# Landmark attention and an MLP on one core: a matrix engine order written in the program, fp32 loads with engine casts, landmark sums by matmul

## The chip, the cores and the metric

One core of a Trainium2 chip runs the whole program. The metric is the device time of one execution in microseconds. A core has a matrix engine (TensorE, "PE" in the rows, with "PEld" for its weight loads), a vector engine (VectorE, "DVE"), a scalar engine (ScalarE, "ACT"), a general engine (GpSimd, "POOL") and a queue engine that issues transfers (SyncE, "SP"). Every engine runs its own instructions in the order in which they stand in its queue and waits for others by semaphores.

## What is computed

For each of 8 batches and 8 heads of 576 tokens with 64 features, the kernel computes a softmax attention through 32 landmarks, which are means over 18 neighbouring tokens each; then a layer norm and an MLP of 512 to 2048 to 512 features on the 4608 token rows.

```python
q_lm = q.reshape(B, H, 32, 18, D).mean(axis=3)
k_lm = k.reshape(B, H, 32, 18, D).mean(axis=3)
A, Bm, C = sm(q, k_lm), sm(q_lm, k_lm), sm(q_lm, k)      # softmax of scaled products
Z = Bm.T / (norm1(Bm) * norminf(Bm) + 1e-6)
for _ in range(6):
    Z = 2 * Z - Z @ Bm @ Z
x = (A @ Z @ C @ v)                                      # heads side by side: 512 features
xn = (x - mean(x)) / sqrt(var(x) + 1e-6) * g_ln
out = x + relu(xn @ w_ch1) @ w_ch2
```

## The kernel before

A batch is one call of `attention_batch` (L197). Its 576 tokens of 8 heads come as two half-sets (`u` = 0, 1) of four heads. The steps are the same for every batch:

- **Loads.** q and k are fetched by GpSimd-issued transfers that cast fp32 to fp16 on the way (`natq` L64, `natk` L68). v comes in fp32 through SyncE into `vstg` (L140) and GpSimd casts it into `natv` (L144). Loads for a batch are issued one batch ahead.
- **Sums and transposes.** VectorE adds each landmark's tokens (`nsk` L209, `nsq` L214, two of each per batch). TensorE transposes the raw q and k in 36 matmuls per batch (`pst`, L188 in the helper `TR`), VectorE copies them to `kT`, `qT` (L226), and a few matmuls bring the sums into the transposed layout (`pslm`), from which VectorE makes `klm` and `qbd` (L239, L242).
- **Landmark block.** `psb` (landmark by landmark products) is exponentiated by ScalarE (`ebm`), normalised by VectorE (`rsum`, `rcr`, `bm`, `bmT`), and gives `pscs`, `pse` and the start `st` of the iteration. `psc` gives the scores of landmarks against all keys, ScalarE exponentiates them into `ect` (12 instructions per batch), and `pscv` multiplies them with v.
- **Iteration.** Six rounds: 8 small matmuls into `psn`, then one VectorE instruction for the next `st` (L321). Then `pszc` and `zcbd` (L331).
- **Token scores and output.** `psa`, exponentiated into `ea`; `psy` (10 matmuls per batch) times `zcbd`, divided by VectorE into the fp32 rows `xblk` (L361).

The MLP works on groups of four blocks of 128 rows (`moe_group`, nine groups): statistics by VectorE (`bn_stats`, L384), `lnv` and `rstd` on ScalarE, the normalised `xn` by GpSimd (L395), 16 transposes into `psxt` with VectorE copies to `xnT` (L401), 64 matmuls of 512 columns into `psh` with 16 ScalarE evictions `hT` (L409), 64 matmuls of 512 columns into `pso`, and per block an addition `ot` on VectorE (L417) and stores.

The matmuls go through the helper `MM`, so nearly all have the line L184. The program writes attention of batch b and then, from batch 2 on, group b-2; a scheduler is free to reorder every engine's queue by what it expects to be ready, TensorE's too. On-chip accumulators are two pools: five buffers shared by all attention steps, and three (`psM`) shared by `psxt`, `psh` and `pso`.

The weight w1 comes in four 1 MB pieces through SyncE and ScalarE scales and casts them (L157); w2 comes cast by a GpSimd-issued transfer (L161).

Of the kernel before, what the change touches and what calls it, by code (L numbers as in the profile page):

```python
# [15 lines left out]
P = 128  # L16
# [3 lines left out]
def kernel(  # L20
# [22 lines left out]
    NCK = SEG // 2  # L43
# [11 lines left out]
    anat = ctx.enter_context(tc.tile_pool(name="anat", bufs=2))  # L55

    def load_qk(b, split):
        natq = anat.tile([P, U, SEG * D], FP16, name="natq", tag="natq")  # L60
        natk = anat.tile([P, H // 2, 9 * D], FP16, name="natk", tag="natk")
        step = 1 if split else U
        for u in range(0, U, step):
            nc.gpsimd.dma_start(  # L64
                out=natq[:, u:u + step, :],
                in_=q[b, 4 * u:4 * (u + step)].rearrange(
                    "(u h) (l j) d -> (h l) u (j d)", u=step, j=SEG))
            nc.gpsimd.dma_start(  # L68
                out=natk[:, 2 * u:2 * (u + step), :],
                in_=k[b, 4 * u:4 * (u + step)].rearrange(  # L70
                    "(r e) (t j) d -> (e t) r (j d)", e=2, j=9))
        return natq, natk

    nat_tiles = {0: load_qk(0, True)}
# [40 lines left out]
    ect_buf = []  # L115
    zcbd_buf = []
    for i in range(NV):
        t = const.tile([P, H // 2, 9, D + 1], FP16, name=f"natv{i}")
        nc.gpsimd.memset(t[:, :, :, D:D + 1], 1.0)
        natv_buf.append(t)  # L120
        ects = []
        zcs = []
        for u in range(U):
            e_ = const.tile([P, SEG, 2, LM], FP16, name=f"ect{i}{u}")
            nc.gpsimd.memset(e_[0:64, :, 1, :], 0.0)
            nc.gpsimd.memset(e_[64:128, :, 0, :], 0.0)
            ects.append(e_)
# [3 lines left out]
        ect_buf.append(ects)  # L131
        zcbd_buf.append(zcs)

    vstage = ctx.enter_context(tc.tile_pool(name="vstage", bufs=2))

    def load_v(b):
        natv = natv_buf[b % NV]
        for r in range(0, H // 2, 2):
            stg = vstage.tile([P, 2, 9, D], FP32, name="vstg", tag="vstg")
            nc.sync.dma_start(  # L140
                out=stg[:],
                in_=v[b, 2 * r:2 * r + 4].rearrange("(r e) (t j) d -> (e t) r j d",
                                                    e=2, j=9))
            nc.gpsimd.tensor_copy(out=natv[:, r:r + 2, :, 0:D], in_=stg[:])  # L144
        return natv

    v_tiles = {0: load_v(0)}

    g_sb = wpool.tile([P, KCH], FP32, name="g_sb")
    nc.sync.dma_start(out=g_sb[:], in_=moe_g_ln.rearrange("(c p) -> p c", p=P))  # L150
    w1_16 = wpool.tile([P, KCH, HID], FP16, name="w1_16")
    w2_16 = wpool.tile([P, MCH, DM], FP16, name="w2_16")
    with tc.tile_pool(name="wstage", bufs=2) as wstage:
        for c in range(KCH):
            stg = wstage.tile([P, HID], FP32, name="w1stg", tag="w1stg")
# [12 lines left out]
    asm = ctx.enter_context(tc.tile_pool(name="asm", bufs=3))

    xpool = ctx.enter_context(tc.tile_pool(name="xpool", bufs=22))  # L170
    mstat = ctx.enter_context(tc.tile_pool(name="mstat", bufs=4))
    mxn = ctx.enter_context(tc.tile_pool(name="mxn", bufs=2))
    mxnT = ctx.enter_context(tc.tile_pool(name="mxnT", bufs=2))
    mhT = ctx.enter_context(tc.tile_pool(name="mhT", bufs=1))
    mout = ctx.enter_context(tc.tile_pool(name="mout", bufs=2))

    ps1 = ctx.enter_context(tc.tile_pool(name="ps1", bufs=5, space=bass.MemoryType.PSUM))
    psM = ctx.enter_context(tc.tile_pool(name="psM", bufs=3, space=bass.MemoryType.PSUM))

    def pt(shape, dtype, name):  # L180
        return ps1.tile(shape, dtype, name=name, tag="p1")

    def MM(o, l, r, rb=0, cb=0, start=True, stop=True, skip=False):
        nc.tensor.matmul(o, l, r, start=start, stop=stop, tile_position=(rb, cb),  # L184
# [277 lines left out]
```

## Time and profile before

| | us |
|---|---|
| median of three runs | 458.29 |
| lowest and highest | 458.02, 458.29 |
| profiled execution, its own time | 456.55 |
| span of the profiled execution | 454.7 |
| TensorE busy in the span | 367.4 |
| VectorE busy | 237.0 |
| ScalarE busy | 141.5 |
| GpSimd busy | 69.1 |
| mean granted TensorE clock | 0.97 of full |

The span is the time from the first to the last instruction of the core; the profiled execution's own time is 1.85 us more. Busy times of engines overlap. A matmul's duration in the rows contains its pipeline, so neighbouring ones overlap, and the pace is read from the starts.

### The profile page before, as it was taken

What the parts mean: (1) busy time and instruction counts of PE and PEld (TensorE: products, weight loads), DVE (VectorE), ACT (ScalarE), POOL (GpSimd) and SP (SyncE); (2) the same over time, 40 slices, a digit from 0 to 9 for tenths busy, and PEclk for the clock granted to TensorE, in tenths of its full rate; (3) what the DMA queues carried; (4) which work ended last, traced back from release to release, by engine and by line L of the source; (5) the groups of instructions that cost most, each with busy time, mean ns of one, the idle gap of its engine ahead of it and who ended that gap; (6) DMA issues with size and microseconds to landing.
All of it is one profiled execution on the core that took longest, in us unless ns stands there. A gap on an engine that the chain in (4) does not pass through costs nothing.

```text
span 454.7 us, 7489 instructions
## 1 busy us (share of the span) xinstructions
PE 367.4 (81%) x2968; PEld 180.1 (40%) x2968; DVE 237.0 (52%) x598; ACT 141.5 (31%) x303; POOL 69.1 (15%) x102
## 2 busy tenths in 40 slices
PE   1124066798995899699978998999899899899995
PEld 1022034354353345334543455346444444444442
DVE  3546679788787673866286726634473201102001
ACT  1333013147103540354025504530552160350520
POOL 8512102312112100320042002000200200200000
PEclk9999998599998999999989999999899999999999
DMA  9999706306226303630270020003000201102002
GB/s 202 326 309 253 192 1 105 106 10 150 76 54 121 105 1 79 120 105 0 72 127 1 2 69 25 2 16 78 1 1 25 69 0 48 46 1 69 25 23 70
DMA packets 20946, 35.08 MB, mean 77 GB/s; under 512 B 3504, under 2 KB 9648, under 8 KB 20400
## 3 DMA queue, kind: packets, MB, share of 16 engines
q1 hardware_dynamic: 12368, 23.08, 16.8%
q0 software_dynamic: 8544, 11.54, 15.1%
q8 instruction: 23, 0.38, 0.3%
q14 instruction: 11, 0.09, 0.1%
HBM read 36.70 MB, written 9.44 MB: 101 GB/s over the span
## 4 chain that ended last, share of the span: by engine, by line
PE 59%; DMA 18%; DVE 11%; issue 6%; ACT 2%; POOL 2%; SPq 0%; POOLq 0%; DVEq 0%
PE pso L184 27%; PE psh L184 23%; DMA natq<-in_q_dram 8%; DMA natk<-in_k_dram 4%; DVE nsq L214 4%; DMA w1stg<-in_moe_w_ch_dram 3%; DVE nsk L209 2%; PE psy L184 2%; DMA vstg<-in_v_dram 2%; PE psn L184 2%; POOL xn L395 2%; PE pst L188 1%; PE psxt L188 1%; DVE kT L226 1%; DVE xnT L401 1%
## 5 line engine op out<-in xcount | busy, mean ns | idle before, releaser
L184 PE MATMUL psh<-xnT,w 128*128 128x512 f16 x576 | 148.9, 390 | 5.3 <-DVE xnT L401 5.3
L184 PE MATMUL pso<-w,hT 128*128 128x512 f16 x576 | 127.9, 379 | 0.0
L409 ACT ACTIVATE hT<-psh 128x512 f16<-128x512 f32 x144 | 86.0, 597 | 125.2 <-PE psh L184 124.6
L417 DVE TENSOR_TENSOR ot<-pso,xblk 128x512 f32<-128x512 f32 x36 | 24.9, 690 | 131.5 <-PE pso L184 128.7
L184 PEld LDWEIGHTS <-hT 128*128 128x128 f16 x576 | 55.6, 98 | 66.0
L184 PEld LDWEIGHTS <-w 128*128 128x128 f16 x576 | 52.0, 99 | 54.5 <-issue 6.8
L395 POOL TENSOR_SCALAR xn<-xblk,rstd,negmr 128x512 f16<-128x512 f32 x36 | 27.5, 770 | 168.5 <-PE psxt L188 165.0
L214 DVE TENSOR_REDUCE nsq<-natq 128x64 f16<-128x1152 f16 x16 | 33.7, 2104 | 16.7 <-DMA natq<-in_q_dram 16.7
L209 DVE TENSOR_REDUCE nsk<-natk 128x128 f32<-128x1152 f16 x16 | 33.7, 2107 | 9.1 <-DMA natk<-in_k_dram 9.1
L296 ACT ACTIVATE ect<-psc 64x192 f16<-64x192 f32 x96 | 31.2, 325 | 21.3 <-PE psc L184 19.7
L188 PE MATMUL pst<-ident,natk 128*128 128x128 f16 x144 | 12.6, 238 | 28.0 <-DMA natk<-in_k_dram 16.1
L361 DVE TENSOR_TENSOR xblk<-psy,rcpd 128x256 f32<-128x256 f32 (+1 forms) x80 | 31.2, 419 | 0.5
L255 ACT ACTIVATE ebm<-psb 128x64 f32<-128x64 f32 x8 | 1.8, 224 | 90.7 <-PE psb L184 90.7
L184 PE MATMUL psn<-st 32*32 32x96 f16 (+1 forms) x384 | 14.6, 216 | 18.0 <-DVE st L308 14.2
L321 DVE SCALAR_TENSOR_TENSOR st<-st,psn 128x192 f16<-128x192 f16 (+1 forms) x48 | 16.4, 342 | 23.8 <-PE psn L184 23.8
L144 POOL CAST natv<-vstg 128x1152 f16<-128x1152 f32 x16 | 18.4, 1150 | 64.4 <-PE pscv L184 48.9
L68 POOL DMA_DIRECT2D natk<-in_k_dram x9 | 6.9, 768 | 117.5 <-PE pst L188 102.4
L384 DVE BATCH_NORM_STATS2 st<-xblk 128x6 f32<-128x512 f32 x36 | 23.4, 667 | 0.0
L188 PEld LDWEIGHTS <-natk 128*128 128x128 f16 x144 | 10.4, 107 | 30.3 <-DMA natk<-in_k_dram 16.4
L184 PEld LDWEIGHTS <-st 32*32 32x32 f16 x384 | 6.5, 91 | 38.9 <-DVE st L321 18.6
L184 PE MATMUL psy<-zcbd,ea 128*128 128x260 f16 (+1 forms) x80 | 18.7, 298 | 2.8 <-ACT ea L346 2.1
L346 ACT ACTIVATE ea<-psa 128x288 f16<-128x288 f32 x32 | 10.5, 417 | 27.8 <-PE psa L184 27.8
(71 smaller groups left out, 275.4 us busy)
## 6 DMA issues: line engine op xcount, KB each, us to landing
vstg<-in_v_dram SPq DMA_DIRECT2D x16, 576.0 KB, 4.4
out_dram<-ot SPq DMA_DIRECT2D x144, 64.0 KB, 1.7
w1stg<-in_moe_w_ch_dram SPq DMA_DIRECT2D x4, 1024.0 KB, 10.1
natq<-in_q_dram POOLq DMA_DIRECT2D x7, 576.0 KB, 7.7
natk<-in_k_dram POOLq DMA_DIRECT2D x7, 576.0 KB, 6.0
w<-in_moe_w_ch_dram POOLq DMA_DIRECT2D x4, 512.0 KB, 24.6
natq<-in_q_dram POOLq DMA_DIRECT2D x2, 288.0 KB, 7.7
natk<-in_k_dram POOLq DMA_DIRECT2D x2, 288.0 KB, 11.4
```

What stands on the lines that cost most here:

```text
L144: nc.gpsimd.tensor_copy(out=natv[:, r:r + 2, :, 0:D], in_=stg[:])
L184: nc.tensor.matmul(o, l, r, start=start, stop=stop, tile_position=(rb, cb), skip_group_check=(skip or cb != 0))
L188: nc.tensor.matmul(o, i_, idn, is_transpose=True, tile_position=(0, 0))
L209: nc.vector.tensor_reduce(out=nsk[:, 2 * u:2 * u + 2, :], in_=natk[:, 2 * u:2 * u + 2, :].rearrange("p r (j d) -> p r d j", j=9), axis=AX. ...
L214: nc.vector.tensor_reduce(out=nsq[:, u, :], in_=natq[:, u, :].rearrange("p (j d) -> p d j", j=SEG), axis=AX.X, op=ALU.add)
L296: nc.scalar.activation(ect[u][sl, 6 * g:6 * g + 6, e, :], psc[sl, :, :, e, :].rearrange("p i s m -> p (i s) m"), AF.Exp, scale=sc_C)
L321: nc.vector.scalar_tensor_tensor(out=stn[:, :, lo:], in0=st[:, :, lo:], scalar=2.0, in1=psn[:, :, lo:], op0=ALU.mult, op1=ALU.subtract)
L361: nc.vector.tensor_tensor(out=xb[ds(pb, n), ds(256 * u, 256)].rearrange("s (h e) -> s h e", e=D), in0=psy[ds(pb, n), :, 0:D], in1=rcpd[ds( ...
L384: nc.vector.bn_stats(out=st6[:], in_=x_blk[4 * g + u][:])
L395: nc.gpsimd.tensor_scalar(out=xn[:], in0=x_blk[4 * g + u][:], scalar1=rstd[:, u:u + 1], scalar2=negmr[:, u:u + 1], op0=ALU.mult, op1=ALU.add)
L409: nc.scalar.activation(hT[:, m, :], psh[:], AF.Relu)
L417: nc.vector.tensor_tensor(out=ot[:], in0=pso[:], in1=x_blk.pop(j)[:], op=ALU.add)
```

## The change

- TensorE's queue and SyncE's loads are kept in the order in which the program writes them (`keep_in_program_order`); the other engines are still ordered by the scheduler. The attention of a batch becomes a generator that stops after each step with a number n; the MLP is a generator that stops after each matmul. Between two attention steps `fill` writes 2n MLP matmuls (n in the rest of batch 1). Batch 0 runs without MLP work; from its second iteration round on each of its steps is followed by a step of batch 1.
- q, k and v all come in fp32 through SyncE into six shared staging buffers, and an engine casts them: in batch 0 VectorE, ScalarE and GpSimd share it, later GpSimd casts all. The fp16 tile has two heads side by side, so that a transpose yields both heads' features on the partitions; the token order of `out` follows from the load (nine residues), so a block is stored by one or two transfers instead of four.
- The landmark sums `nsq`, `nsk` on VectorE and the `pslm` matmuls go; instead each of the 36 fp16 pieces per batch is multiplied once more, with a 64-column 0/1 matrix (`pss`).
- `psc` has 36 matmuls of 64 columns on half of the array's columns instead of 18 of 128 columns, and its exponentials are 2 instructions per batch on 128 partitions instead of 12 on 64. `pscv` has 72 matmuls on 64 by 32 tiles of the array instead of 36 on 128 by 64. `psa` moves in between the iteration rounds. `psy` of both half-sets goes into one two-bank buffer, with one division per block.
- w1 comes in eight 512 KB pieces after the loads of batches 0 and 1, cast in 32 instructions; w2 follows. Statistics are taken as each block is done.
- Attention accumulators: one single buffer for the small steps, two of two banks for the large ones; `psM` still has three.

The core of the diff:

```diff
+    def MM(o, l, r, rb=0, cb=0, start=True, stop=True, skip=False):
+        tc.keep_in_program_order(
+            nc.tensor.matmul(o, l, r, start=start, stop=stop, tile_position=(rb, cb),
+                             skip_group_check=(skip or cb != 0)))
+    def load(src, b, u):
+        t = stage.tile([P, 2, NJ, D], FP32, name="stg", tag="stg")
+        tc.keep_in_program_order(nc.sync.dma_start(
...
+    def load_qk(b, engines):
...
+            t = nat.tile([P, NJ, 2, D], FP16, name="nat", tag="nat")
+            cast(eng, t[:].rearrange("p j r d -> p r j d"), tiles[key][:])
...
+    nat_tiles = {0: load_qk(0, ("dve", "act", "pool", "dve"))}
...
+    v_tiles = {0: load_v(0, ("pool", "pool"))}
+    nat_tiles[1] = load_qk(1, ("pool", "pool", "pool", "pool"))
+    v_tiles[1] = load_v(1, ("pool", "pool"))
...
+    wstage = ctx.enter_context(tc.tile_pool(name="wstage", bufs=2))
+    W1N = 256
...
-            nc.vector.tensor_reduce(
-                out=nsk[:, 2 * u:2 * u + 2, :],
...
-                nc.vector.tensor_reduce(
-                    out=nsq[:, u, :],
...
+                pst = p2([P, NJ, P], FP16, "pst")
+                for j in range(NJ):
+                    TR(pst[:, j, :], n16[:, j, :, :].rearrange("p r d -> p (r d)"), ident16[:])
+                for j in range(NJ):
+                    MM(pss[:, i, u, :], n16[:, j, :, :].rearrange("p r d -> p (r d)"), pm16[:],
+                       start=(j == 0), stop=(j == NJ - 1), skip=True)
...
+                yield 2
...
+            psc = p2([P, NJ, 64], FP32, "psc")
+            for j in range(NJ):
+                for e in range(2):
+                    MM(psc[ds(64 * e, 64), j, :], xT["k", u][:, j, ds(64 * e, 64)],
+                       qbd[:, 2 * u + e, :, :], cb=64 * e)
...
+                    MM(pscv[ds(32 * h, 32), u, :], ect[u][rows, j, ds(32 * r, 32)],
+                       natv[rows, 2 * u + r, j, :], rb=64 * e, cb=32 * h,
+                       start=(j == 0), stop=(j == NJ - 1), skip=True)
...
+    def fill(n):
+        for _ in range(n):
+            if not next(stream, False):
+                return
+    a0, a1 = attention(0), attention(1)
+    for i, _ in enumerate(a0):
+        if i == 5:
+            for w in range(HID // W1N):
+                load_w1(w)
+            for m in range(0, MCH, 4):
+                load_w2(m)
+        if i >= 9:
+            next(a1)
+    for b in range(1, B):
+        if b + 1 < B:
+            nat_tiles[b + 1] = load_qk(b + 1, ("pool",) * 4)
+            v_tiles[b + 1] = load_v(b + 1, ("pool",) * 2)
+        gen = a1 if b == 1 else attention(b)
+        for n in gen:
+            fill(n if b == 1 else 2 * n)
+    for _ in stream:
+        pass
```

**VectorE at the landmark block of a middle batch.** In the kernel before, the reduces of the next batch (`nsk`, `nsq`) stand between the short instructions of the landmark block:

```order
L261 TENSOR_TENSOR bm_1624<-ebm,rcr 128x64
L391 SCALAR_TENSOR_TENSOR negmr<-mvg,rstd 128x4
L209 TENSOR_REDUCE nsk<-natk 128x128
L264 STREAM_TRANSPOSE bmT<-bm_1624 128x64
L274 TENSOR_REDUCE cmx<-pscs 128x2
L214 TENSOR_REDUCE nsq<-natq 128x64
L275 TENSOR_SCALAR cmx<-cmx 128x2
L209 TENSOR_REDUCE nsk<-natk 128x128
L278 RECIPROCAL cinv<-cmx 128x2
L307 RECIPROCAL rcv<-pscv 128x1
L214 TENSOR_REDUCE nsq<-natq 128x64
L280 TENSOR_TENSOR st<-pse,cinv 128x2x32
```

The same engine and place in the changed kernel:

```order
L231 COPY xT<-pst 128x1152 x4
L237 CAST klm<-pss 128x128
L239 TENSOR_TENSOR qbd<-pss,mask_97 128x256
L256 TENSOR_REDUCE rsum<-ebm 128x2
L258 RECIPROCAL rcr<-rsum 128x2
L260 TENSOR_TENSOR bm_1921<-ebm,rcr 128x64
L263 STREAM_TRANSPOSE bmT<-bm_1921 128x64
L286 TENSOR_REDUCE cmx<-psse 128x2
L287 TENSOR_SCALAR cmx<-cmx 128x2
L290 RECIPROCAL cinv<-cmx 128x2
L292 TENSOR_TENSOR st<-psse,cinv 128x2x32
```

The four long reduces are gone from between `bm` and `st`; four copies `xT` stand ahead of the block.

**ScalarE in the first two batches.** Before, the four casts of w1 come first, then the attention of batches 0 and 1 (`ebm`, `ect`, `ea`), then the first group's `lnv` and `rstd`:

```order
L157 ACTIVATE w_16_129<-w1stg,g_sb 128x2048 x4
L255 ACTIVATE ebm<-psb 128x64
L296 ACTIVATE ect_96<-psc 64x6x32 x6
L296 ACTIVATE ect_101<-psc 64x6x32 x6
L346 ACTIVATE ea<-psa 128x288 x4
L255 ACTIVATE ebm<-psb 128x64
L296 ACTIVATE ect_108<-psc 64x6x32 x6
L296 ACTIVATE ect_113<-psc 64x6x32 x6
L387 ACTIVATE lnv<-mvg,eps_ln 128x4
L389 ACTIVATE rstd<-lnv 128x4
```

In the changed kernel, from the landmark block of batch 1 on:

```order
L254 ACTIVATE ebm<-psb 128x64
L275 ACTIVATE ect<-psc 128x576
L172 ACTIVATE w_16_147<-w1stg,g_sb 128x256 x8
L275 ACTIVATE ect<-psc 128x576
L172 ACTIVATE w_16_147<-w1stg,g_sb 128x256 x8
L338 ACTIVATE ea<-psa 128x576 x2
L393 ACTIVATE lnv<-mvg,eps_ln 128x4
L172 ACTIVATE w_16_147<-w1stg,g_sb 128x256 x8
L395 ACTIVATE rstd<-lnv 128x4
L172 ACTIVATE w_16_147<-w1stg,g_sb 128x256 x8
L448 ACTIVATE hT<-psh 128x512 x7
```

The casts of w1 now stand among batch 1's exponentials, and the first group's `rstd` stands behind three quarters of them.

## Rows read from the trace of the kernel before

**Rows 1.** Page: TensorE's line; busy tenths and bandwidth in 40 slices of 11.4 us.

```profile
PE 367.4 (81%) x2968; PEld 180.1 (40%) x2968; DVE 237.0 (52%) x598; ACT 141.5 (31%) x303; POOL 69.1 (15%) x102
...
PE   1124066798995899699978998999899899899995
...
GB/s 202 326 309 253 192 1 105 106 10 150 76 54 121 105 1 79 120 105 0 72 127 1 2 69 25 2 16 78 1 1 25 69 0 48 46 1 69 25 23 70
```

**Rows 2.** Chain that ended last, in time: start us, us, what; head to end.

```profile
35.75 17.62 DMA natk<-in_k_dram
...
132.43 2.01 PE pst L188 x36
...
184.18 6.34 DMA natq<-in_q_dram
190.55 2.11 DVE nsq L214
192.74 2.04 DVE nsk L209
194.91 2.04 DVE nsq L214
...
271.87 0.69 DVE ot L417
...
314.70 0.69 DVE ot L417
...
391.42 13.97 PE psh L184 x64
405.39 13.81 PE pso L184 x64
...
449.92 0.69 DVE ot L417
```

**Rows 3.** Page, costliest groups: count, then busy us and mean ns of one.

```profile
L214 DVE TENSOR_REDUCE nsq<-natq 128x64 f16<-128x1152 f16 x16 | 33.7, 2104 | 16.7 <-DMA natq<-in_q_dram 16.7
L209 DVE TENSOR_REDUCE nsk<-natk 128x128 f32<-128x1152 f16 x16 | 33.7, 2107 | 9.1 <-DMA natk<-in_k_dram 9.1
...
L361 DVE TENSOR_TENSOR xblk<-psy,rcpd 128x256 f32<-128x256 f32 (+1 forms) x80 | 31.2, 419 | 0.5
...
L144 POOL CAST natv<-vstg 128x1152 f16<-128x1152 f32 x16 | 18.4, 1150 | 64.4 <-PE pscv L184 48.9
...
L384 DVE BATCH_NORM_STATS2 st<-xblk 128x6 f32<-128x512 f32 x36 | 23.4, 667 | 0.0
```

**Rows 4.** TensorE timeline: start us, us, matmuls; first `psh`, and inside one batch.

```profile
85.68 1.01 PE L184 MATMUL psh<-xnT,w 128*128 128x512 f16 x2 [0.24 <-DVE xnT L401]
...
86.90 2.74 PE L184 MATMUL psh<-xnT,w 128*128 128x512 f16 x6
...
195.80 0.38 PE L184 MATMUL pscv<-natv,ect 128*64 128x65 f16 x11
196.11 0.82 PE L184 MATMUL psh<-xnT,w 128*128 128x512 f16 x3
...
198.90 0.82 PE L184 MATMUL psh<-xnT,w 128*128 128x512 f16 x3
199.65 0.26 PE L184 MATMUL psn<-st 32*32 32x96 f16 x8
199.85 0.82 PE L184 MATMUL psh<-xnT,w 128*128 128x512 f16 x3
...
203.58 0.44 PE L184 MATMUL psa<-qT,klm 64*32 64x288 f16 x16
203.95 0.39 PE L184 MATMUL psh<-xnT,w 128*128 128x512 f16 x1
```

**Rows 5.** Groups by line: w1's casts and the copies after the MLP transposes.

```profile
L401 DVE COPY xnT<-psxt 128x512 f16<-128x512 f16 x36 | 14.1, 413 | 1.8 <-PE psxt L188 1.8
...
L157 ACT ACTIVATE w<-w1stg,g_sb 128x2048 f16<-128x2048 f32 x4 | 8.0, 2001 | 20.0 <-DMA w1stg<-in_moe_w_ch_dram 20.0
```

More of the change, by code (lines that the diff above doesn't have):

```diff
@@ L42 @@
     U = H // 4
[L43 removed]
+    NJ = 9
     scale_qk = 1.0 / (D ** 0.5)
@@ L54 @@
     wpool = ctx.enter_context(tc.tile_pool(name="wpool", bufs=1))
[L55 to L72, printed above, removed]
@@ L178 @@
     psM = ctx.enter_context(tc.tile_pool(name="psM", bufs=3, space=bass.MemoryType.PSUM))
[L180 to L184, printed above, removed]
-                         skip_group_check=(skip or cb != 0))
-    def TR(o, i_, idn):
-        nc.tensor.matmul(o, i_, idn, is_transpose=True, tile_position=(0, 0))
@@ new lines, in attention, with p1, p2 @@
+        pool1, tag1 = (psM, "pm") if b == 1 else (ps1, "p1")
+        def p1(shape, name):
+            return pool1.tile(shape, FP32, name=name, tag=tag1)
+        def p2(shape, dtype, name):
+            return ps2.tile(shape, dtype, name=name, tag="p2")
+        pss = p1([P, 2, U, 64], "pss")
+        xT = {}
+        for u in range(U):
+            for i, nm in enumerate(("q", "k")):
+                n16 = nt[nm, u]
+                pst = p2([P, NJ, P], FP16, "pst")
[4 more added lines that the diff above has]
+                       start=(j == 0), stop=(j == NJ - 1), skip=True)
+                t = aprep.tile([P, NJ, P], FP16, name="xT", tag="xT")
+                if b < 2 and nm == "k":
+                    nc.scalar.copy(t[:], pst[:])
+                else:
+                    nc.vector.tensor_copy(out=t[:], in_=pst[:])
+                xT[nm, u] = t
+                yield 2
@@ new lines, in attention @@
+        klm = asm.tile([P, U, 64], FP16, name="klm", tag="klm")
+        nc.vector.tensor_copy(out=klm[:], in_=pss[:, 1, :, :])
+        qbd = asm.tile([P, U * 2, 2, LM], FP16, name="qbd", tag="qbd")
+        nc.vector.tensor_tensor(
+            out=qbd[:],
+            in0=pss[:, 0, :, :].rearrange("p u (e l) -> p (u e) l", e=2)[:, :, None, :]
+            .broadcast_to([P, U * 2, 2, LM]),
+            in1=mask2[:, None, :, None].broadcast_to([P, U * 2, 2, LM]), op=ALU.mult)
+        yield 2
@@ new lines, in attention @@
+            for j in range(NJ):
+                for h in range(4):
+                    r, e = divmod(h, 2)
+                    rows = ds(64 * e, 64)
+                    MM(pscv[ds(32 * h, 32), u, :], ect[u][rows, j, ds(32 * r, 32)],
+                       natv[rows, 2 * u + r, j, :], rb=64 * e, cb=32 * h,
+                       start=(j == 0), stop=(j == NJ - 1), skip=True)
+        rcv = asm.tile([P, U], FP32, name="rcv", tag="rcv")
+        nc.vector.reciprocal(out=rcv[:], in_=pscv[:, :, D])
```

369 lines of the change are left out of this document (178 added, 191 removed).

## The prediction

> **What bounds the kernel now.** I read the page first. TensorE is busy 81% of the span, but its digits in the 40 slices stay low up to the seventh slice and are eights and nines afterwards [rows 1]: there are two stages with different limits. The timeline of TensorE dates the border. The first MLP matmul (`psh`) starts at 85.68 us [rows 4], and the last `ot` begins at 449.92 [rows 2], so the span of 454.7 is 85.7 of head, 364.2 in which the 1152 large matmuls run, and 4.8 of last store.
>
> The chain of waits, in time, says what holds each stage. In the head it is transfers and VectorE: one `natk` step of the chain alone is 17.62 us [rows 2]. In the middle, at 184.18, a batch stands on its `natq` load for 6.34 us and then on three VectorE reduces of 2.1 us each, in front of the few short instructions that TensorE waits for [rows 2]. Where nothing waits, the chain is `psh` and `pso` alone: 64 in 13.97 and 64 in 13.81, that is 218 and 216 ns each [rows 2]. Later batches are free of the reduces; from the `ot` at 271.87 to that at 314.70 one period with 128 large matmuls takes 42.8 us [rows 2].
>
> **Large matmuls.** They are not changed: 576 x 0.218 + 576 x 0.216 = 250.0 us, all on the path.
>
> **What TensorE does per batch after the change.** The prices are taken from pace in the rows (start to start).
> - `pst` is still 36, in 2.01 [rows 2]: 2.0.
> - `pss` adds 36 of 64 columns, each with its own 128-column weights like a `pst`. At `pst`'s pace 2.0. Below, no matmul with fresh weights in these rows is faster than `pscv`'s 28 ns (11 in 0.31) [rows 4]: 1.0. I take 2.0, since the weights are those of `pst`.
> - `psc` is 36 on half-width weights, nearest to `pscv` in shape: 28 to 35 ns, 1.2 (bounds 1.0 and, at `pst`'s pace, 2.0).
> - `pscv` is 72 on 64 by 32 tiles. Nearest is `psa`, on the same tiles: 16 of 288 columns in 0.37, 23 ns each [rows 4]; at 28 ns it is 2.0. I take 1.9 (bounds 1.7 and 2.0).
> - six `psn` rounds. Three `psh` and one round of 8 repeat every 0.95 us (198.90 to 199.85); less 3 x 0.218 a round costs 0.30 with both changes of tile shape [rows 4]. Six: 1.8.
> - `psa` has the same columns as before: 0.4. `psb`, `psse`, `pszc`, 25 small ones, like a round of `psn` each: 0.9.
> - `psy`, 10 of 260 columns at the large pace per column 1.1; I add 0.1 for each of five insertions: 1.6.
>
> Sum 11.8 a batch (10.3 to 13.0 with the bounds). A batch's fill is 130 stops of the MLP generator, about one group: 126 large ones and 4 steps of transposes.
>
> **The stretch with MLP work.** It starts in the same state as before: batch 0 done, batch 1 in its last iteration rounds. 250.0 for the large ones; 128 MLP transposes at `pst`'s pace 7.2; six batches 6 x 11.8 = 70.8; the rest of batch 1, 2.3; the first eight or so `psh` run at 0.44 us (6 in 2.74) [rows 4] and not 0.22: 2. The 16 transposes of a group now stand in one piece and have only three `psM` buffers, one still held by a `pso`; they go at the pace of the copies `xnT`, 0.41 each [rows 5], behind an `ot`: about 1 us idle, eight times, 8. Sum 340.3.
>
> **What hides the rest.** The VectorE reduces (32 of 2.1) [rows 3] go, 67 us of VectorE. What is late next is the chain behind each step, which must fit under 4 to 8 large matmuls (0.87 to 1.74). `klm` and `qbd` need about 0.9 under 1.74; a round's `st` 0.8 under 2.0; `zcbd` two instructions, about 1.4 under 1.74. In the `psy` phase VectorE needs a division (2 x 0.42, less one start), 0.67 of statistics [rows 3], 0.17 and 0.17, about 1.75 per block, against 1.55 on TensorE; five blocks and two `ot` make 10 us against 7.8, a lag that the two `psy` buffers and the next batch's start take up. GpSimd's six casts of 1.15 [rows 3] and four `xn` make 10 us in 42. SyncE's loads of the batch after next stand ahead of the stores, and the stores wait for `ot`; the loads have a whole batch of lead. I allow 1 us a batch for what does not fit (0 to 3): 6. The stretch: 346 against 364.
>
> **The head.** Twelve loads of 576 KB go out at once on one queue; at the 310 GB/s of the second and third slice [rows 1] each takes 1.9 us. The fourth is in at 11, batch 1's last k at 22. A cast (1.15), 18 matmuls and the landmark block bring the first `psn` to about 22. The rounds carry batch 1's transposes between them (2 us each at half the later pace) and end at 32; batch 1's first `ect` is at 35. From there ScalarE's order decides. Eight casts of 256 columns take 0.37 each by w1's 2.0 for 2048 [rows 5], 3 us per pair of pieces; a piece lands some 4 us after its buffer is free. Pairs are cast by 38, 44 and 50; `rstd` follows the third, `xn` and the transposes take 3: first `psh` at **53**. If pieces land in 2 us it is 46; if the attention chain is 8 us later than I have it, or w2's transfer shares the bandwidth all along, 65.
>
> **Sum.** 53 + 346 + 4.8 = 404 span, 406 with the 1.85 around it, against 456.55. The median of the runs stands 1.7 above the profiled execution: 407.5, which I round to **408**.
>
> **A rule against it.** A round of `psn` between two runs of `psh` costs 0.30 us [rows 4], hardly more than its own eight matmuls at `pscv`'s pace (0.22). The Trainium skill ("TensorEngine Tiling (Array Packing)", Key Properties) says that a change of tiling mode drains TensorE. By the rows the sum is 408; by that rule taken at full price it is the first rival's 423.
>
> **Rivals.**
> - *Drain.* If each of ten insertions with small tiles costs two drains of 0.17 (a large matmul lasts 0.38 and is issued every 0.22), that is 3.4 a batch, 0.9 of which I have in: 15 us more, 423. For it: there are 20 such changes per batch. Against it: the 0.30 above. 7%.
> - *Order gives nothing.* The scheduler's period without reduces is already 42.8 [rows 2], and mine is 42. If TensorE's fixed order loses by rigidity what the reduces' end gives back, only the head remains: 458 - 33 = 425. 9%.
> - *The head stays.* If w1, behind batch 1's work on ScalarE and with two buffers, brings the first `psh` to 70 or more, 425 to 440. 8%.
> - *Slower.* In a fixed order a late producer stops all of TensorE, not one step. There are 26 hand-overs a batch, 156 in six batches. If VectorE stands behind an `ot` (0.69) or statistics (0.67) [rows 3] at each, so that each waits on average 0.32 us, 50 us are lost and the time is 458; at 0.4, 470. Half that gives 433. For it: VectorE's lag of 2 us in the `psy` phase. Against: the covers above are larger than the chains. 3% beyond 459, 4% around 433.
> - *Faster.* If `pss`, `psc` and `pscv` overlap on the array and no hand-over waits, a batch costs 9.5, and 6 x 3.3 go: 384 to 388. 9%.
>
> **How the numbers follow.** My forecast has 60%, with its own range 392 to 424 from the bounds (head 46 to 65, batch 10.3 to 13.0, waits 0 to 3). With drain, order and the lower part of the late head, 388 to 432 holds 8 in 10. A measurement of this kernel tells 0.2% (0.9 us) from no change. Faster 96%, same 1%, slower 3%.
>
> **What would show it.** The first `psh` of the new profile between 46 and 65; the last `pso` about 346 after it; no reduce of 2 us; a period from batch to batch of 42; idle TensorE of about 1 us at each 16 `psxt`; `psn` rounds still at 0.3 beyond the `psh` pace. I am wrong if TensorE idles before `psb`, `psn` or `psy` in every batch, if the first `psh` is past 70, or if `pss` or `pscv` run at more than 60 ns each.

## The result and the profile after

| | before | after |
|---|---|---|
| median, us | 458.29 (458.02 to 464.06) | 394.25 (391.23 to 395.44) |
| profiled execution, its own time | 456.55 | 391.23 |
| its span | 454.7 | 389.5 |
| first `psh` begins | 85.7 | 52.0 |
| last `ot` begins | 449.9 | 374.7 |
| from there to the end of the span | 4.8 | 14.9 |

The ratio is 0.857, 95% interval 0.848 to 0.865. The forecast was 408 with 388 to 432 around it: the side and the range are right, the middle is 14 us too high. That difference is in the main the sum of two misses of opposite sign. The stretch between the first `psh` and the last `ot` is 322.6 us and not 346, and the end behind it is 14.9 us and not 4.8.

The page of the kernel after, the lines that answer to [rows 1]: busy time by engine, then in 40 slices of 9.7 us TensorE's busy tenths, its granted clock in tenths, and bandwidth:

```profile
PE 344.7 (89%) x3528; PEld 175.7 (45%) x3528; DVE 170.0 (44%) x431; ACT 129.7 (33%) x240; POOL 82.1 (21%) x100
...
PE   1796299799999999999999999999999999999940
...
PEclk9998679999999999999999999999999999999985
...
GB/s 294 395 216 245 161 334 393 74 15 53 316 95 29 45 339 65 21 51 354 52 46 33 364 34 26 51 34 3 29 60 22 14 51 44 14 72 23 14 51 42
```

From the ninth slice on TensorE's digit is a nine up to the last two slices; the seven just before them, from 68 to 78 us, holds a wait of 2.5 us that comes up again below. In [rows 1] most of these digits are eights and nines, with a five, a six and sevens among them. VectorE went from 237 to 170 us, the 67 us of the reduces [rows 3]. The last two slices hold a hint: bandwidth of 51 and 42 GB/s while TensorE falls to 4 and 0.

The chain of waits (start us, us, what), to be held against [rows 2]:

```profile
33.86 5.23 DMA w1stg<-in_moe_w_ch_dram
...
39.11 3.31 ACT w L172 x8
...
42.43 4.32 DMA w1stg<-in_moe_w_ch_dram
...
46.77 1.71 ACT w L172 x4
...
317.75 13.81 PE psh L61 x64
...
360.80 13.83 PE pso L61 x64
```

The reduces of [rows 2] are gone from it, and of the loads of q and k only the first is left (6.29 us, from 1.81 on). The head ends with w1's pieces and their casts, and behind it the chain is nearly all TensorE. The large matmuls kept their price: 13.81/64 = 216 ns.

TensorE's timeline in a middle batch (start us, us, matmuls, the idle time before them in brackets), against [rows 4]:

```profile
107.36 0.43 PE L61 MATMUL pss<-pm,nat 128*128 128x64 f16 x9
107.62 1.89 PE L61 MATMUL psh<-xnT,w 128*128 128x512 f16 x8
109.44 0.22 PE L61 MATMUL psb<-klm,qbd 64*32 64x32 f16 x8
109.59 0.76 PE L61 MATMUL psc<-qbd,xT 128*64 128x64 f16 x36
110.29 1.90 PE L61 MATMUL psh<-xnT,w 128*128 128x512 f16 x8
...
114.13 0.76 PE L61 MATMUL pscv<-natv,ect 64*32 64x65 f16 x72
114.82 0.82 PE L61 MATMUL psh<-xnT,w 128*128 128x512 f16 x3
...
121.41 0.27 PE L61 MATMUL psn<-st 32*32 32x96 f16 x8
121.61 1.90 PE L61 MATMUL pso<-w,hT 128*128 128x512 f16 x8
123.44 0.26 PE L61 MATMUL psn<-st 32*32 32x96 f16 x8
...
124.29 0.61 PE L66 MATMUL psxt<-ident,xn 128*128 128x128 f16 x8
125.24 0.71 PE L66 MATMUL psxt<-ident,xn 128*128 128x128 f16 x8 [0.34 <-DVE ot L459]
125.90 0.38 PE L61 MATMUL pso<-w,hT 128*128 128x512 f16 x1
...
147.57 0.60 PE L61 MATMUL psc<-qbd,xT 128*64 128x64 f16 x26
```

From `psc` to `psc`, 109.59 to 147.57, a period is 37.98 us, with 126 large matmuls in it. The only idle time that the timeline marks in it is the 0.34 in the middle of the 16 `psxt`.

TensorE's waits from 52 to 375 us (engine and line, waited for: us in total, times, longest):

```profile
PE psse L61 <- DVE bmT L263: 2.5, 1, 2.5
PE psxt L66 <- DVE ot L459: 2.3, 7, 0.3
```

All the others together are 1.1 us. So of 322.6 us TensorE stands idle for 6.

### The profile page after: what moved, and what is told of

The parts are those of the page before. It is cut to its first block, busy times and chain, and to the rows that moved or that the text cites. A ratio compares the mean times of both kernels' runs of the same rounds, so it can differ in the third digit from the quotient of the medians.

```text
span 389.5 us, 8220 instructions
## 1 busy us (share of the span) xinstructions
PE 344.7 (89%) x3528; PEld 175.7 (45%) x3528; DVE 170.0 (44%) x431; ACT 129.7 (33%) x240; POOL 82.1 (21%) x100
## 4 chain that ended last, share of the span: by engine, by line
PE 82%; DVE 6%; DMA 4%; ACT 2%; issue 1%; POOL 1%; SPq 0%
PE pso L61 33%; PE psh L61 31%; PE pst L66 5%; DMA w1stg<-in_moe_w_ch_dram 2%; PE pss L61 2%; PE psn L61 2%; PE psy L61 2%; PE psxt L66 2%; ACT w L172 2%; DMA stg<-in_q_dram 2%; PE psa L61 2%; DVE ot L459 1%; DVE bm L260 1%; PE pscv L61 1%; PE psc L61 1%
## 5 line engine op out<-in xcount | busy, mean ns | idle before, releaser
L448 ACT ACTIVATE hT<-psh 128x512 f16<-128x512 f32 x144 | 85.7, 597 | 159.8 <-PE psh L61 159.8
L61 PE MATMUL psh<-xnT,w 128*128 128x512 f16 x576 | 137.5, 380 | 0.2 <-DVE xnT L427 0.2
L61 PEld LDWEIGHTS <-hT 128*128 128x128 f16 x576 | 53.1, 98 | 60.2 <-issue 3.3
L459 DVE TENSOR_TENSOR ot<-pso,xblk 128x512 f32<-128x512 f32 x36 | 24.8, 689 | 80.5 <-PE pso L61 80.5
L82 POOL CAST nat<-stg 128x1152 f16<-128x1152 f32 x29 | 32.9, 1148 | 88.1 <-DMA stg<-in_q_dram 49.8
L324 DVE SCALAR_TENSOR_TENSOR st<-st,psn 128x192 f16<-128x192 f16 (+1 forms) x48 | 16.4, 342 | 48.6 <-PE psn L61 48.6
L66 PE MATMUL pst<-ident,nat 128*128 128x128 f16 x288 | 24.6, 239 | 6.7 <-DVE nat L80 5.4
L231 DVE COPY xT<-pst 128x1152 f16<-128x1152 f16 x28 | 21.1, 755 | 19.2 <-PE pst L66 19.2
L367 DVE TENSOR_TENSOR xblk<-psy,rcpd 128x512 f32<-128x512 f32 (+1 forms) x40 | 27.3, 684 | 0.7
L66 PEld LDWEIGHTS <-nat 128*128 128x128 f16 x288 | 20.9, 107 | 13.5 <-DVE nat L80 5.4
L82 POOL CAST natv<-stg 128x1152 f16<-128x1152 f32 x16 | 18.3, 1153 | 3.7 <-DMA stg<-in_v_dram 3.7
L66 PE MATMUL psxt<-ident,xn 128*128 128x128 f16 x144 | 12.9, 228 | 6.5 <-DVE xn L402 4.1
L61 PE MATMUL pss<-pm,nat 128*128 128x64 f16 x288 | 15.4, 204 | 3.5 <-POOL pm L114 3.5
L338 ACT ACTIVATE ea<-psa 128x576 f16<-128x576 f32 x16 | 10.4, 650 | 18.3 <-PE psa L61 18.3
L172 ACT ACTIVATE w<-w1stg,g_sb 128x256 f16<-128x256 f32 x32 | 13.4, 496 | 5.1 <-DMA w1stg<-in_moe_w_ch_dram 5.1
L61 PEld LDWEIGHTS <-nat 128*128 128x128 f16 x288 | 13.3, 106 | 3.7 <-issue 3.7
L66 PEld LDWEIGHTS <-xn 128*128 128x128 f16 x144 | 9.9, 101 | 10.3 <-DVE xn L402 4.3
```

What stands on the lines that cost most here:

```text
L66: nc.tensor.matmul(o, i_, idn, is_transpose=True, tile_position=(0, 0)))
L82: nc.gpsimd.tensor_copy(out=out_, in_=in_)
L172: nc.scalar.activation(w1_16[:, c, ts(i, W1N)], stg[:, c, :], AF.Copy, scale=g_sb[:, c:c + 1])
L231: nc.vector.tensor_copy(out=t[:], in_=pst[:])
L324: nc.vector.scalar_tensor_tensor(out=stn[:, :, lo:], in0=st[:, :, lo:], scalar=2.0, in1=psn[:, :, lo:], op0=ALU.mult, op1=ALU.subtract)
L338: nc.scalar.activation(t[:], psa[:].rearrange("p j t -> p (j t)"), AF.Exp, scale=sc_A)
```

## Experiments

All experiments start from the kernel after. This table has what their traces give: first `psh`, last `ot`, the stretch between, and the tail from the last `ot` to the end of the span. They are of one execution per run, whose own time lies up to 2.6 us from the median. The runs were made on several chips; the kernel before, measured beside each, took 458.1 to 459.4 us, so about 1 us between runs of different chips means nothing.

| run | median us | first `psh` | last `ot` | stretch | tail |
|---|---|---|---|---|---|
| after, unaltered (a0_control) | 394.58 | 52.4 | 377.7 | 325.3 | 14.8 |
| store by 64 rows (e1_store) | 386.53 | 54.2 | 380.5 | 326.3 | 5.0 |
| `pscv` tile by tile (e4_pscv_onetile) | 400.70 | 53.1 | 381.5 | 328.4 | 14.9 |
| `bm` on ScalarE (e5_bm_act) | 394.08 | 53.2 | 377.8 | 324.6 | 14.8 |
| blocks, free order (e2_blocks_free) | 397.91 | 57.2 | 380.8 | 323.6 | 14.9 |
| blocks, fixed order (e2_blocks_fixed) | 469.25 | 60.4 | 452.4 | 392.0 | 14.8 |
| sums on VectorE (e3_dve_sums) | 443.19 | 54.5 | 427.9 | 373.4 | 14.9 |
| w1 casts shared (e6_w1_pool) | 381.86 | 45.2 | 366.5 | 321.3 | 14.9 |
| `bm` and `cmx` on ScalarE (e8_bm_cmx) | 390.70 | 54.1 | 374.1 | 320.0 | 14.9 |
| store and w1 (e7_store_w1) | 371.33 | 44.6 | 365.3 | 320.6 | 5.0 |
| five buffers (e10_wstage5) | 395.50 | 58.5 | 379.3 | 320.8 | 14.8 |
| all of them (e9_all) | 374.75 | 48.6 | 370.1 | 321.5 | 5.1 |

The control expects only the time of the kernel after:

> The changed kernel once more, unaltered, on the chip of the three runs beside it, as their yardstick. Expected: a span near 389.5 us, first psh near 52.0, last ot near 374.7, and 12 to 15 us from the start of the last ot to the end.

It gave 394.58 (394.24 to 395.18), ratio 0.859 [0.857, 0.862]. Its stretch is 2.7 us longer than that of the profile above: TensorE waits as long in both (5.9 us), but is busy for 319.4 us and not 316.7. So differences of that size between two single profiles mean nothing; the medians are closer.

### The tail: one transfer for 64 rows

```diff
-            nc.sync.dma_start(out=rows[t0 // 64:(t0 + n) // 64], in_=ot[ds(p0, n), :])
+            for i in range(n // 64):
+                nc.sync.dma_start(out=rows[t0 // 64 + i], in_=ot[ds(p0 + 64 * i, 64), :])
```

> Each output block is stored by one transfer per residue (64 rows of 2 KB) instead of one transfer for both residues (2 x 64 rows). In the changed kernel the transfers after the last ot run at 51 GB/s and 12.4 us are waited for; before, with 32 rows per transfer, the last ot began 4.8 us before the end. Theory A, the shape of the transfer (outermost size 2) keeps it on few DMA engines: the end comes about 5 us after the last ot begins, so 9 to 10 us less, 384 to 385 us by the median of 394. Theory B, the last stores are slow because 256 KB blocks leave in a burst: the same bytes leave in the same time, within 1 us of the yardstick.

386.53 us (384.81 to 387.38), ratio 0.841 [0.838, 0.845]: 8.05 less than the control on the same chip, and the tail is 5.0. The waits of SyncE's queue at the end, first of the kernel after, then of this one:

```profile
SPq L517 <- DMA out_dram<-ot: 12.4, 1, 12.4
```

```profile
SPq L518 <- DMA out_dram<-ot: 1.8, 1, 1.8
```

The bandwidth behind these waits, in 40 slices from 374 to 390 us of the kernel after and from 370 to 386 us of this one:

```profile
GB/s 51 51 51 51 51 51 51 51 51 51 51 51 51 51 51 51 51 51 51 51 51 46 51 51 51 51 51 51 51 51 51 51 51 51 36 0 0 0 0 0
```

```profile
GB/s 0 0 0 0 36 205 225 174 16 0 0 0 0 128 184 225 118 0 0 0 0 0 189 195 215 56 0 0 0 0 56 200 128 225 67 0 0 0 0 0
```

A store of 256 KB, written as two residues of 64 rows, moves at 51 GB/s; two of 128 KB move at about 200. At 51 GB/s a block needs 5.1 us. With attention in between, a block comes every 9.5 us (37.98/4) and the slow store is hidden; in the last group, with no attention left, a block comes every 3.5 us (13.83/4), the stores pile up, and the pile stands behind the last `ot`. The Trainium skill ("DMA: Bandwidth & Descriptors", Why a DMA increments its semaphore by 16 and not by 1) says that a transfer is spread over the largest number of engines up to 16 that divides the slowest dimension of both its patterns. That number is 2 for the one form and 16 for the other. The traces agree: the mean share of the DMA engines is 0.1 under the first row, and reaches 0.9 under the second.

### Is it the array or the scheduler: `pscv` tile by tile

```diff
-            for j in range(NJ):
-                for h in range(4):
+            for h in range(4):
+                for j in range(NJ):
```

> Only the order of the 72 pscv matmuls changes: all nine of one head in a row on one 64x32 tile of the array, instead of the four heads in turn on four tiles. In the changed kernel 72 take 0.69 us (9.6 ns each), before 28 ns each on 128x64. Theory A, the low price comes from neighbours on different tiles running beside each other: without it about 28 ns each, 2.0 us per batch, 1.3 us more for each of eight batches, 8 to 12 us more in all. Theory B, the price is that of a small matmul whatever its neighbour: within 1 us of the yardstick.

400.70 us (398.14 to 401.73), ratio 0.872 [0.869, 0.876], 6.1 more than the control. The same 72 matmuls in a middle batch, with successive ones on the same 64 by 32 tile:

```profile
116.28 1.70 PE L61 MATMUL pscv<-natv,ect 64*32 64x65 f16 x72
```

1.70 us against 0.76: 0.94 more per batch, 5.6 in the six batches that have MLP work around them. The profile bears it out: its stretch is 5.8 us longer than that of the first profile (328.4 against 322.6), at a granted clock of 1.00 in both. That is less than the 8 to 12 us expected, since a matmul costs some 23 ns from start to start and not 28. At the pace of the large matmuls, 216 ns for 512 columns, 65 columns need 27 ns. The 9.6 ns of the kernel after are therefore possible only with several tiles at work at the same time, and they are if successive matmuls go to different ones. (The edit also lets successive matmuls add into the same accumulator; the large ones do that too and keep their pace.) That is the rival "faster" of the prediction, and it is what `pscv`'s price there left out.

### What the fixed order is worth: two kernels with blocks

In both, the attention of a batch is written whole and its MLP work behind it; in the first TensorE's order is left to the scheduler, in the second it stays as written.

```diff
+        total = 0
         for n in attention(b):
-            fill(n if b == 1 else 2 * n)
+            total += n if b == 1 else 2 * n
+        fill(total)
```

> The written order of TensorE is undone: a whole attention batch is written, then its share of MLP work, and the scheduler orders TensorE as in the kernel before. Casts, sums, tiles and stores stay as changed. Theory A (the gain of the stretch comes from cheaper attention matmuls and from the reduces that left VectorE; the interleaving by hand adds little): the scheduler interleaves as it did before, 2 to 6 us more than the changed kernel. Theory B (the written order is what fills TensorE): the stretch goes back towards 42 us per batch, 4 us for each of six batches and more in the first, 20 to 30 us more.

> The same writing without MLP matmuls between attention steps, but TensorE kept in that order: every hand-over from attention to VectorE or ScalarE is then waited for by TensorE. Both theories: much slower. The waits of a batch by the prediction's chains: nine short ones of 0.5 to 1.5 us around psb, psse, pscv and zcbd, six rounds of 0.5, the psy steps at VectorE's 1.75 instead of 1.55: 12 to 15 us per batch, 70 to 100 us more than the changed kernel. It prices what the fill hides.

Free: 397.91 us (395.58 to 399.86), ratio 0.866 [0.862, 0.870]. Fixed blocks: 469.25 (467.02 to 470.61), ratio 1.021 [1.018, 1.025], some 2% slower than the kernel before. In the fixed blocks TensorE waits at each step, and its granted clock is below 0.9 in 17 of the 40 slices:

```profile
PE psy L61 <- DVE xblk L367: 14.8, 12, 1.5
PE psn L61 <- DVE st L324: 8.3, 18, 0.5
...
PEclk9876577599958996699969985999589999999995
```

So the fill is worth some 67 us (392.0 against 325.3). About 45 of them are waits of TensorE (50.6 in this stretch, 5.9 in the control's); the other 23 are the same matmuls taking longer (342.1 us busy against 319.4) at a granted clock of 0.88 in the stretch instead of 0.99. But the scheduler finds a filling as good as the written one: its stretch is 323.6 against 325.3, and the 3.3 us that it loses are in the head, where the first `psh` comes at 57.2 and not 52.4. With the new steps the gain over before's 364 is thus there under either order, as long as the work is interleaved.

### Sums back on VectorE

```diff
-                for j in range(NJ):
-                    MM(pss[:, i, u, :], n16[:, j, :, :].rearrange("p r d -> p (r d)"), pm16[:],
-                       start=(j == 0), stop=(j == NJ - 1), skip=True)
+                nsum = asm.tile([P, 2 * D], FP16, name="nsum", tag="nsum")
+                with nc.allow_low_precision("segment sums feed fp16 matmuls"):
+                    nc.vector.tensor_reduce(
+                        out=nsum[:], in_=n16[:].rearrange("p j r d -> p (r d) j"),
+                        axis=AX.X, op=ALU.add)
+                MM(pss[:, i, u, :], nsum[:], pm16[:], skip=True)
```

> The landmark sums go back to VectorE: per quarter batch one reduce of 1152 fp16 values to 128 (2.1 us by the rows of the kernel before) and one pss matmul instead of nine. Theory A (the sums by TensorE are worth it because VectorE stood in front of TensorE): per step VectorE then has 0.76 + 2.1 against 1.4 on TensorE, 1.4 us of waiting at each of four steps in six batches, less a slack of some 2 us per batch, 15 to 25 us more. Theory B (with the fixed order VectorE has room, 21 us busy of 38): the 1.0 us of pss per batch is saved, 4 to 6 us less.

443.19 us (442.24 to 444.50), ratio 0.965 [0.963, 0.968]: 48.6 more than the control, twice the upper end of what was expected. The group of the reduces, and TensorE's three longest waits from 54 to 428 us:

```profile
L226 DVE TENSOR_REDUCE nsum<-nat 128x128 f16<-128x1152 f16 x32 | 67.6, 2112 | 24.9 <-POOL nat L82 24.8
...
PE pst L66 <- DVE xT L234: 23.5, 5, 6.3
PE psse L61 <- DVE bmT L266: 11.3, 5, 4.6
PE pss L61 <- DVE nsum L226: 3.4, 2, 2.0
```

The expectation counted the reduces' own time. VectorE's queue is in order too: a reduce that waits for GpSimd's cast (24.8 us in all) holds the copies `xT` behind it, and the fixed TensorE order holds all large matmuls behind the next `pst`. The waits of TensorE in the stretch come to 45.6 us, 39.7 more than in the control. The other 8 of the 48 are longer busy time (327.9 us against 319.4, although `pss` has fewer matmuls), with a granted clock of 0.94 in the stretch instead of 0.99. Under the fixed order the move of the sums to TensorE (`pss`, 1.06 us a batch by the rows above) is therefore worth 48.6 us; sums on VectorE with the order left to the scheduler were not tried.

### The one wait of 2.5 us: `bm`

VectorE, then GpSimd, in the kernel after, just before that wait:

```profile
69.41 0.22 DVE L256 TENSOR_REDUCE rsum<-ebm 128x2 f32<-128x64 f32 x1 [1.13 <-ACT ebm L254]
69.66 0.17 DVE L258 RECIPROCAL rcr<-rsum 128x2 f32<-128x2 f32 x1
69.86 3.95 DVE L260 TENSOR_TENSOR bm<-ebm,rcr 128x64 f16<-128x64 f32 x1
```

```profile
67.13 4.42 POOL L82 CAST nat<-stg 128x1152 f16<-128x1152 f32 x4
71.50 2.24 POOL L82 CAST natv<-stg 128x1152 f16<-128x1152 f32 x2
```

An instruction that elsewhere takes 0.22 us lasts until GpSimd's run of six casts is over (73.74). The reduce and the reciprocal beside it are not held.

```diff
-        nc.vector.tensor_tensor(out=bm16[:], in0=ebm[:],
-                                in1=rcr[:, :, None].broadcast_to([P, U, LM]), op=ALU.mult)
+        for u in range(U):
+            nc.scalar.activation(bm16[:, u, :], ebm[:, u, :], AF.Copy, scale=rcr[:, u:u + 1])
```

> The normalisation bm (fp32 in on-chip memory, 64 columns) moves from VectorE to two ScalarE instructions. In the changed kernel one bm lasts 3.95 us, from 69.86 to the end of a row of GpSimd casts, and TensorE then idles 2.5 us before psse; the other seven are shorter (median 0.54). Theory A, this VectorE operation waits for GpSimd: the idle time before psse of batch 2 goes, 2.5 to 3.5 us less. Theory B, what waits is VectorE as such: the next VectorE instruction in its place is as long, no gain.

394.08 us (393.73 to 394.35), ratio 0.858 [0.855, 0.861]: nothing. The wait before `psse` is gone, but now TensorE waits 1.84 us before a `psn`; 40 us later the trace has this, VectorE and then GpSimd:

```profile
112.70 4.88 DVE L287 TENSOR_SCALAR cmx<-cmx 128x2 f32<-128x2 f32 x1
```

```profile
109.09 3.01 POOL L402 TENSOR_SCALAR xn<-xblk,rstd,negmr 128x512 f16<-128x512 f32 x4
112.05 3.32 POOL L82 CAST nat<-stg 128x1152 f16<-128x1152 f32 x3
115.32 2.24 POOL L82 CAST natv<-stg 128x1152 f16<-128x1152 f32 x2
```

Another instruction of VectorE met the next run and lasted until its end, 117.56. The run with both on ScalarE tells whether that is the reason:

```diff
-        nc.vector.tensor_scalar(out=cmx[:], in0=cmx[:], scalar1=1e-6, scalar2=None,
-                                op0=ALU.add)
+        nc.scalar.activation(cmx[:], cmx[:], AF.Identity, bias=eps_ln[:])
```

> Both VectorE instructions that were seen to last out a GpSimd run go to ScalarE: `bm` (3.95 us in the changed kernel's trace, 69.86 to 73.81, while GpSimd's casts ran without a gap to 73.74) and the addition of 1e-6 to `cmx` (4.88 us, 112.70 to 117.58, GpSimd's run ending at 117.56, in the run with `bm` alone on ScalarE). Theory A: a VectorE instruction of this kind waits for the end of the GpSimd run that it meets, and with `bm` alone moved the wait was only met one instruction later, so with both moved it is gone: last `ot` some 4 us after its place in the control is undercut (the 2.5 us wait and about 1.4 us of slow TensorE clock after it): 390 to 391.5 us against the control's 394.6, no wait over 1 us between 60 and 370 us. Theory B: the gain is eaten by the added ScalarE instructions, wherever the VectorE ones stand: 394 us again. Theory C: another VectorE instruction (`zcbd`, `st`) meets the run in their place: a new one of over 3 us, 393 to 395 us.

390.70 us (389.70 to 391.32), ratio 0.853 [0.850, 0.855]: Theory A. No wait over 0.4 us is left after the first `psh`, and the stretch is 320.0. GpSimd's run still covers the same place of the batch, and VectorE goes on inside it:

```profile
111.60 3.33 POOL L82 CAST nat<-stg 128x1152 f16<-128x1152 f32 x3
114.87 2.25 POOL L82 CAST natv<-stg 128x1152 f16<-128x1152 f32 x2
```

```profile
112.55 0.17 DVE L289 RECIPROCAL cinv<-cmx 128x2 f32<-128x2 f32 x1 [0.36 <-ACT cmx L287]
112.75 0.22 DVE L291 TENSOR_TENSOR st<-psse,cinv 128x64 f16<-128x64 f32 x1
```

So it was not a shift of the run that removed the wait. Part is given back in the head (54.1), where the reciprocal `cinv` waits 5.85 us for the moved addition, which stands behind w1's casts on ScalarE:

```profile
42.17 0.17 DVE L289 RECIPROCAL cinv<-cmx 128x2 f32<-128x2 f32 x1 [5.85 <-ACT cmx L287]
```

The Trainium skill ("SBUF — State Buffer", Who interferes with whom) names this: VectorE and GpSimd share a pair of ports to SBUF, the on-chip memory of the tiles; an instruction of VectorE with two inputs from SBUF needs it, a `tensor_scalar` can use it, a reduce never does, and whoever is first has it for the whole instruction. Which instructions were held and which not agrees with it: `bm` has two inputs from SBUF and `cmx` is a `tensor_scalar`, while `st` above, with one of its two inputs in an accumulator, took its usual 0.22. The page speaks of one instruction; here the hold lasted through the rest of a run, three further casts for `bm` and four for `cmx`.

### The head: w1

Half of w1's casts to GpSimd, and five staging buffers in place of two:

```diff
-    wstage = ctx.enter_context(tc.tile_pool(name="wstage", bufs=2))
+    wstage = ctx.enter_context(tc.tile_pool(name="wstage", bufs=5))
...
+            if c < 2:
+                nc.scalar.activation(w1_16[:, c, ts(i, W1N)], stg[:, c, :], AF.Copy,
+                                     scale=g_sb[:, c:c + 1])
+            else:
+                nc.gpsimd.tensor_scalar(out=w1_16[:, c, ts(i, W1N)], in0=stg[:, c, :],
+                                        scalar1=g_sb[:, c:c + 1], scalar2=None, op0=ALU.mult)
```

> Five staging buffers for w1 instead of two, and half of w1's casts on GpSimd, which is idle from 30 to 50 us. In the changed kernel the chain before the first psh (52.0) is two w1 transfers of 5.2 and 4.3 us with 3.3 us of casts behind each. Theory A, w1's round trips through two buffers set the start of the MLP: first psh at 46 to 48, 4 to 6 us less. Theory B, the attention of batches 0 and 1 or the bandwidth sets it: first psh stays at 51 to 52, no gain.

381.86 us (380.36 to 383.15), ratio 0.830 [0.827, 0.833]: 12.7 less than the control, twice the upper end of what was expected. The chain around 40 us no longer has a transfer of w1:

```profile
38.08 0.79 ACT w L173 x2
```

The first `psh` comes 7.2 us earlier (45.2). A further 4.0 us come from the stretch: the `psse` wait of 2.5 us does not occur, though `bm` was left on VectorE, and neither do the slow `psh` that followed it in the control (1.4 us; last section). GpSimd's casts now have gaps between them: this `bm` begins at 64.34, between a cast that ends at 63.61 and one that starts at 64.69, and takes 0.23 us. The longest of the eight took 0.80, which fits the reading above. These two make 11.2 us; the medians, of runs on different chips, are 12.7 apart.

The buffers alone, `bufs=5` with all casts on ScalarE:

> The run with w1's casts shared changed two things, five staging buffers instead of two and half of the casts on GpSimd, and took 12.7 us off. Here the buffers are alone, ScalarE casts all of w1. In the control the chain of the head has one transfer of a piece (6.79 us) behind a buffer and 1.70, 3.30 and 3.19 us of casts on ScalarE. Theory A, the buffers matter: the transfers leave the chain, the casts remain, first `psh` between 46 and 49, 384 to 390 us. Theory B, ScalarE's casts matter: ScalarE has the same 12 us of casts in the way of `ect`, `ea` and `rstd`, only sooner; first `psh` at 51 to 53, 392 to 395 us.

395.50 us (394.68 to 395.85), ratio 0.861 [0.858, 0.865]: nothing is gained, and the first `psh` comes at 58.5, later than either theory had it. ScalarE's timeline in the head and TensorE's longest wait:

```profile
30.50 8.07 ACT L172 ACTIVATE w<-w1stg,g_sb 128x256 f16<-128x256 f32 x20
40.72 1.71 ACT L172 ACTIVATE w<-w1stg,g_sb 128x256 f16<-128x256 f32 x4 [2.15 <-DMA w1stg<-in_moe_w_ch_dram]
44.44 3.30 ACT L172 ACTIVATE w<-w1stg,g_sb 128x256 f16<-128x256 f32 x8 [2.02 <-DMA w1stg<-in_moe_w_ch_dram]
...
PE pscv L61 <- ACT ect L275: 13.6, 1, 13.6
```

All 32 casts, with the waits for their pieces, stand in one row on ScalarE, ahead of batch 1's second `ect` (47.65), and its attention chain stops for 13.6 us. So the 7.2 us need the casts on GpSimd; what the buffers add to that was not tried.

### Together

> The two edits that paid, together: one output transfer per 64 rows, and five staging buffers for `w1` with half of its casts on GpSimd. If they add: 381.9 less the 8.0 to 9.9 us that the store gave (386.5 against 394.6 us; tail 5.0 against 14.8 us) = 372 to 374 us, first `psh` at 45, last `ot` at 366.5, tail 5. If the store's transfers get into the way of the head of the next loads: 376 to 380 us.

371.33 us (370.56 to 372.03), ratio 0.810 [0.808, 0.813]: the two edits add (381.86 less 8.05 is 373.8), and this is the fastest kernel of the study, 23 us under the kernel after.

> The former with `bm` and the addition to `cmx` on ScalarE as well. In the run with the moved `w1` casts TensorE had no wait over 1.2 us after the first `psh`, so there is nothing left to win there: Theory A of the run before gives 372 to 374 us, the same within 1 us. If ScalarE's three instructions more per batch cost anything, it shows here alone: 375 to 377 us.

374.75 us (373.99 to 376.89), ratio 0.818 [0.815, 0.820]: 3.4 more. The stretch is the same (321.5 and 320.6); the loss is the head. GpSimd's queue there, with w2's transfers ahead of the first two `xn`:

```profile
42.61 3.19 POOL L180 DMA_DIRECT2D w<-in_moe_w_ch_dram  x4
45.83 1.52 POOL L405 TENSOR_SCALAR xn<-xblk,rstd,negmr 128x512 f16<-128x512 f32 x2
```

With three more instructions on ScalarE the scheduler put w2's four transfer issues ahead of these `xn`; without them (e7) the `xn` start at 41.46 and the issues at 45.21. TensorE's `psxt` wait 3.59 us for it. So what cost time was not ScalarE's work, as the expectation had it, but a changed order on a third engine.

## Why the prediction was right or wrong

**Head: right.** 53 was said, 52.0 came, and by the steps named: casts of w1's pairs done by 38, 44 and 50 were said, ScalarE's timeline has the first three pairs cast by 35.4, 42.4 and 48.5; a piece some 4 us after its buffer is free, measured 4.3 and 5.2. The price of a cast there, 0.37 us "by w1's 2.0 for 2048", does not follow from its row, which gives 0.25 by columns; measured are 0.41 (8 in 3.30). The head's gain of 33.7 us is half of all, and no run undoes the loads alone or w1's place alone, so how it divides between them is not shown.

**Large matmuls: right.** 250.0 said; 1152 x 0.216 = 248.8.

**Attention per batch: 11.8 said, 9.2 measured.** The period of 37.98 less 126 x 0.216 and less 1.61 for the `psxt` leaves 9.2. By steps, from starts to starts, and with the 0.1 that a run of large matmuls loses at its end when small tiles follow (8 in 1.83 instead of 1.73):

| step | said | measured |
|---|---|---|
| `pst` | 2.0 | 2.0 |
| `pss` | 2.0 | 1.06 |
| `psc` | 1.2 | 0.70 |
| `pscv` | 1.9 | 0.79 |
| six `psn` | 1.8 | 1.8 |
| `psa` | 0.4 | 0.72 |
| `psb`, `psse`, `pszc` | 0.9 | 0.81 |
| `psy` | 1.6 | 1.34 |

The failed terms are `pss`, `psc` and `pscv`, 2.55 of the 2.6. For `pss` the lower bound of 1.0 was the right one: nine matmuls of 64 columns with fresh weights go in 0.265, 29 ns each, half of a `pst`. `psc` goes at 19 ns and `pscv` at 9.6 ns, below the lower bounds of 28 and 23 ns. The error is in the reading of [rows 4]: no matmul with fresh weights was said to be faster than 28 ns, yet the `psa` of the next lines goes at 23 ns, and with 288 columns, which by the large matmuls' pace need 122 ns alone. In the kernel before it went round eight tiles, so tiles at work at the same time could be seen there; the prediction took its 23 ns as the price of a matmul whatever its columns. e4 shows that this is the reason for `pscv`; for `psc` it was not tried. `psa` missed the other way (0.4 said, 0.72 measured): it now goes round four tiles at a time, in two pieces, which may be why, and was not tried either. The sum lies below the 10.3 that had been given as the lower end (the bounds of the steps add up to 10.4 and 12.7).

**Waits: 6 said, 3.6 measured,** 2.5 of it the one at `bm` and 1.1 four short ones. `psxt`: 1 us idle each said, 0.33 measured, and 16 of them take 1.61; 15.2 said for all, 12.9 measured. With 6 x 2.6 = 15.6 for attention, 2.4 for the waits, 2.3 for these and 1.2 for the large matmuls, 21.5 of the stretch's 23.4 us are found.

**No drain of the rival's size.** A round of `psn` with 8 `pso` repeats every 2.03 us (121.41 to 123.44); less 8 x 0.216 that is 0.30, the price taken from [rows 4]. The rival of 423 by drains is out.

**Order gives nothing:** half true, as the blocks in free order show. A fixed order written by hand is no better than the scheduler's within the stretch. But the period did not stay at 42.8 as that rival had it, since the steps got cheaper.

**Tail: wrong, by 10 us.** The failed step is the 4.8 of the sum, taken over from before although the change rewrites the stores; 14.9 were measured. The part on the change even says that a block is stored by one or two transfers instead of four; the prediction counted them and never asked what one would take. With a tail of 5 the kernel stands at 386 (e1): the miss of the stretch alone is 22 us, and the tail hid half of it. 386 lies outside the forecast's 388 to 432 and in the 384 to 388 of the rival "faster", whose reason, steps that overlap on the array, came true in the main. That 394 lies inside is luck. The step from the profiled execution to the median, 1.7 said, was 3.0.

## What to carry to other kernels

A change that rewrites a transfer has a price at the end of the kernel, where nothing hides it: look at the rate of the last store, and not only at the number of stores. Small matmuls on tiles of the array should go round the tiles, and their price is not that of one matmul in another row: compare it with its columns at the large matmuls' pace, and a price below that shows tiles at work side by side. An instruction that lasts far longer than its like (least, median and largest duration of a group show it) should be held against the other engine's run that ends at the same moment before it is moved elsewhere; moved alone, its wait is met by the next one.

## What the runs showed of the hardware

- A store of 256 KB over two residues of 64 rows ran at 51 GB/s; in halves of 64 rows about 200 GB/s.
- `bm` took 3.95 us and `cmx` 4.88 us instead of 0.22 and 0.17, up to 0.07 and 0.02 us after the end of an unbroken GpSimd run of several instructions; reduces and reciprocals in the same run took their usual time.
- 72 matmuls of 65 columns on tiles of 64 by 32 take 0.76 us when successive ones are on different tiles and 1.70 us when they are on the same. In the kernel before, 16 of 288 columns went round eight such tiles in 0.37 us.
- In the control the same `psse` wait (2.52 us) was followed by eight `psh` in 3.28 us, where others take 1.89; the granted clock from 70 to 90 us was 0.91. In the profile of the kernel after, the wait of 2.53 had no such sequel (eight in 1.89, granted clock 1.00 in the same window). What decides it stays open.
